# All expert weights from SP's queue, and a new order for the last third of a delta-rule and soft-MoE kernel

## The chip, the cores and the metric

The kernel runs on one core of one Trainium2 chip. The time is device microseconds of that core. Before the change three runs gave 293.0, 293.39 and 295.69 us, so the median is 293.39 us. One more execution was recorded by the hardware profiler; it took 296.5 us.

## The reference

Two blocks are computed one after the other, all in float32. The first is a delta-rule attention with a state of 48 by 48 for each of 4 x 8 heads, over 768 time steps:

```python
y[:, :, t] = np.einsum('bhd,bhde->bhe', q[:, :, t], state)
v_old = np.einsum('bhde,bhd->bhe', state, kt)          # kt: k normalised by its length
state = state + bt[:, :, :, None] * np.einsum('bhd,bhe->bhde', kt, vt - v_old)
```

Its output, laid out as 3072 rows of 384, is the input `x` of a soft mixture of 8 experts with 4 slots each:

```python
logits = x @ phi                                        # 3072 x 32
d = softmax(logits, axis=0); c = softmax(logits, axis=1)
slot_input = (d.T @ x).reshape(E, S_per_e, D)           # 8 x 4 x 384
for e in range(E):
    slot_out[e] = np.maximum(slot_input[e] @ w1[e], 0) @ w2[e]   # w1 384x1024, w2 1024x384
out = c @ slot_out.reshape(32, D)                       # 3072 x 384
```

The weights `w1` and `w2` are 12.58 MB each (8 x 384 x 1024 x 4 bytes).

## The kernel before, in words

**Tiling.** The 768 steps are cut into 12 chunks of 64 (n = 0 to 11). A chunk holds all 32 heads, with 64 time steps on each half of the 128 partitions. Two chunks form a pair g (0 to 5).

**Stages of a chunk.** `load` (L412) and `load_q` (L421) bring k, v and q in; a `load` is two operations of five DMAs each, one of 96 KB and four of 24 KB. `prep` turns k and q (L473) and forms the Gram blocks (L504). `invert(g)` inverts the triangular systems of a pair on VectorE and GpSimd: it starts with a spread (L563), runs 15 pairs of a multiplication and a subtraction (both recorded at the helper's line L277), and ends with two transposes, `back` (L626) and `backt` (L632). `join(g)` merges blocks with four products on TensorE, called p1 to p4 here (L716, L716, L761, L716), with copies between: `mask` (L687), `swap` (L671 on VectorE or GpSimd, L669 on ScalarE), `fix16` (L733), two `wide` (L739, L741), `zbadd` and `fix32` (L770).

**The recurrence.** `step(n)` scales v (`scale_v`, L277), multiplies k by the state (`ks`, L821), subtracts (`rest`, L827), and multiplies by the joined inverse (the product `w`, L840, interleaved with L782, the second half of the previous chunk's output). `uev` copies the result out of PSUM, `sup` (L867) adds it to the state and two `sev` copy the state to SBUF. `query` (L791) is the previous chunk's first half of output. `yev` copies a chunk's output to SBUF, `route` turns it (L902) and copies it. All copies out of PSUM stand at L281 when ScalarE does them and at L283 on VectorE. For n = 11 the second half of the output is a product of its own, `au` (L782 alone).

**Routing.** `pair(g)` forms the logits (`lg`, L920), a running maximum (L928 to L931), exponentials (L935), the slots' sums (L953, accumulated at L958), and the softmax over experts (L962 to L984). After the last pair a merge (L1050 to L1074) gives the slots' inputs `slb`.

**Experts and output.** `first(1)` and `first(0)` multiply by w1 (L1090, four groups of 24 matmuls), with relu (L1099) and transposes (L1106). `second(0)` and `second(1)` multiply by w2 for the two halves of the columns (L1123; eight groups of 16 matmuls each). After each half, `comb` (L1142) multiplies with the combine weights; a copy and a `put` (L1150) follow. A put is two DMAs of 96 KB; each half has 12 puts.

**What sets the order.** Nothing is scheduled at build time. Every function only records operations in a list (`pl.op`), numbered 0 to 1163. `Plan.run` then issues them in the order of the list `ORDER`, each on the engine that the string `ALTS` picks among the alternatives given to `pl.op`, and with its buffers at the columns of SBUF or the banks of PSUM that the list `PLACE` gives. So an engine's queue is the subsequence of `ORDER` that falls to it, and a later use of a column waits for the earlier one. The weights (25.2 MB) do not fit beside the attention's tiles, so most weight loads go to columns that an attention tile used before, and wait until its last reader is done.

**Weight loads.** w1 is 24 operations of two DMAs (256 KB each, L1029); w2 is 32 operations of two DMAs (192 KB each, L1040). Of the 56 operations 39 are issued on SP's queue and 17 on GpSimd's (POOL): w1 operations 1013, 1016, 1017, 1020, 1023, 1028, 1030, 1035 and w2 operations 1043, 1047, 1052, 1054, 1056, 1057, 1058, 1062, 1068. Six w2 operations go to columns that w1 of experts 4 to 7 held, and so wait for `first(1)`.

DMAs that SP and ScalarE issue share eight completion semaphores, taken in turn; a DMA waits until the eighth DMA before it has landed. GpSimd's DMAs have eight of their own.

Of the kernel before, what the change touches and what calls it, by code (L numbers as in the profile page):

```python
# [113 lines left out]
    "0010021211010001100200000000000000000001010000000000001000000000010000101000000000000000010100000011"  # L114
    "1000001000100001010000010100000000000110000000010000000110100000000211010100011000000000000000000000"
    "0000000000000000010000000000100000000001000000000000000000000111000000000100000011000010000000000011"
    "1100000000000000000000000000002022100001110110100000000000010000000000000000000000000000000100000000"
    "0000000100000000000000000000000000000000000011000000110100100010000000000000100100001000100000000010"
    "0000000000001100110010010000101000010000000100010000101011100010000010000000000000010000000000000000"
    "0000001010010012000000020011000000000000010201210010011000100002"  # L120
)


class Buf:


# [70 lines left out]
def kernel(  # L197
# [823 lines left out]
    for e in range(E):  # L1021
        for kk in range(NKT):
            w1b[e, kk] = t = done.pop(0) if done else pl.buf(F)
            pl.tag = ("w1", e)

            def go(q, e=e, kk=kk, t=t):
                s = moe_w1[e].rearrange("(p k) f -> p k f", k=NKT)
                for x in H2:
                    ENG[q].dma_start(out=A(t)[:, 512 * x:512 * x + 512], in_=s[:, kk, 512 * x:512 * x + 512])  # L1029
            pl.soft = [chain[8]]  # L1030
            pl.op(dq(0.8, 1.2, None), None, go, w=[t], bus=1.5, nd=2)
# [150 lines left out]
```

## Time and profile before

| | |
|---|---|
| median of the runs | 293.39 us |
| the profiled execution | 296.5 us, of which 294.8 us lie between its first and last instruction (the span) |
| PE (TensorE) busy | 227.0 us, 77% of the span, 6252 matmuls |
| DVE (VectorE) busy | 200.2 us, 68% |
| ACT (ScalarE) busy | 145.2 us, 49% |
| POOL (GpSimd) busy | 139.4 us, 47% |
| DMA | 45.13 MB, mean 153 GB/s |
| the chain that ended last | PE 39%, DVE 25%, issue 12%, ACT 9%, POOL 7% of the span |

The page gives times in microseconds from the span's first instruction. PEld is TensorE's weight load. A name with q (SPq, ACTq) is an engine's queue issuing a DMA. "Issue" in the chain is time in which an engine waited for nothing that the profile shows. A row of the chain reads: start, duration, engine, where the result goes, line, and the number of instructions merged. A row of the timeline adds the operation, the shapes, and in brackets the idle time before it with what ended it.

### The profile page before, as it was taken

The numbers are of one execution on the slowest core, as the hardware profiler recorded it, in microseconds if no ns is written. First come the engines' busy times: TensorE is split into PE (matmuls) and PEld (weight loads), VectorE is DVE, ScalarE is ACT, GpSimd is POOL, SyncE is SP. The second block draws the span as 40 slices with busy tenths as digits, with TensorE's granted clock in tenths as the row PEclk, the third lists the DMA queues.
The fourth block names the chain that finished last, engine by engine and source line by source line (L and its number), as shares of the span: only waits on it lengthen the run. The fifth ranks groups of instructions, "written<-read, shape, count | busy, mean of one in ns | idle before, by whom it ended". The sixth has DMA issues, their size and how long they took to land.

```text
span 294.8 us, 14440 instructions
## 1 busy us (share of the span) xinstructions
PE 227.0 (77%) x6252; PEld 183.3 (62%) x6252; DVE 200.2 (68%) x504; ACT 145.2 (49%) x325; POOL 139.4 (47%) x225
## 2 busy tenths in 40 slices
PE   0784788993879887798879977698756978999950
PEld 0563687872768776687667766576655864266640
DVE  4668979979877669778699889785664657113130
ACT  1253486784758356659736778473212432230321
POOL 8998468355483373226762545562730410200460
PEclk9997589999599999999999999999997999999985
DMA  8989642643432361335554607777795699990887
GB/s 138 159 153 188 103 79 59 120 79 58 84 61 52 59 113 24 59 63 117 128 93 111 168 5 226 193 195 221 208 362 186 199 359 374 349 332 4 219 224 201
DMA packets 81519, 45.13 MB, mean 153 GB/s; under 512 B 63520, under 2 KB 74704, under 8 KB 81456
## 3 DMA queue, kind: packets, MB, share of 16 engines
q1 hardware_dynamic: 72704, 30.28, 42.8%
q0 software_dynamic: 5232, 12.56, 15.7%
q10 hardware_dynamic: 3520, 1.38, 2.1%
q8 instruction: 49, 0.80, 1.2%
q14 instruction: 14, 0.11, 0.1%
HBM read 39.47 MB, written 4.72 MB: 150 GB/s over the span
## 4 chain that ended last, share of the span: by engine, by line
PE 39%; DVE 25%; issue 12%; ACT 9%; POOL 7%; DMA 3%; SPq 3%; DVEq 0%; POOLq 0%; ACTq 0%
DVE sb L277 9%; PE pb L716 6%; ACT sb L281 5%; POOL sb L277 5%; PE pb L473 4%; PE pb L1090 4%; PE pb L1123 3%; PE pb L504 3%; PE pb L902 3%; PE pb L782 2%; PE pb L821 2%; PE pb L791 2%; PE pb L867 2%; DMA sb<-in_k_dram 2%; DVE sb L283 2%
## 5 line engine op out<-in xcount | busy, mean ns | idle before, releaser
L281 ACT ACTIVATE sb<-pb 128x512 f32<-128x512 f32 (+5 forms) x144 | 76.0, 560 | 90.9 <-PE pb L473 23.2
L277 POOL TENSOR_TENSOR sb<-sb 128x256 f32<-128x256 f32 (+10 forms) x89 | 64.0, 728 | 66.8 <-DVE sb L277 33.9
L277 DVE TENSOR_TENSOR sb<-sb 128x126 f32<-128x126 f32 (+10 forms) x153 | 54.0, 355 | 11.2 <-POOL sb L277 6.8
L473 PE MATMUL pb<-sb 128*128 128x128 f32 x192 | 33.5, 323 | 15.1 <-DVE sb L329 8.1
L283 DVE COPY sb<-pb 128x512 f32<-128x512 f32 (+5 forms) x43 | 26.2, 618 | 26.0 <-PE pb L473 5.4
L473 PEld LDWEIGHTS pb<-sb 128*128 128x128 f32 x192 | 25.4, 164 | 19.5 <-issue 10.5
L716 PE MATMUL pb<-sb 64*64 64x64 f32 x1152 | 27.5, 232 | 12.3 <-DVE sb L277 4.7
L716 PEld LDWEIGHTS pb<-sb 64*64 64x64 f32 x1152 | 24.3, 144 | 16.0 <-issue 8.0
L504 PE MATMUL pb<-sb 64*64 64x128 f32 x768 | 27.2, 280 | 5.8 <-ACT sb L281 3.3
L840 PE MATMUL pb<-sb 64*64 64x48 f32 x768 | 26.5, 219 | 4.8 <-DVE sb L770 1.8
L840 PEld LDWEIGHTS pb<-sb 64*64 64x64 f32 x768 | 24.4, 135 | 7.6 <-DVE sb L770 2.4
L782 PE MATMUL pb<-sb 64*64 64x48 f32 x768 | 26.3, 219 | 2.2 <-issue 2.1
L504 PEld LDWEIGHTS pb<-sb 64*64 64x64 f32 x768 | 21.9, 136 | 9.1 <-ACT sb L281 4.7
L782 PEld LDWEIGHTS pb<-sb 64*64 64x64 f32 x768 | 24.2, 135 | 2.6 <-issue 2.5
L1040 POOL DMA_DIRECT2D sb<-in_moe_w_dram x18 | 9.7, 542 | 33.6 <-PE pb L953 16.1
L821 PE MATMUL pb<-sb 128*64 128x96 f32 x352 | 18.1, 250 | 3.6 <-ACT sb L281 1.3
L412 POOL DMA_DIRECT2D sb<-in_k_dram x35 | 19.6, 568 | 0.7 <-DVE sb L341 0.7
L1150 POOL DMA_DIRECT2D out_dram<-sb x14 | 8.4, 607 | 23.9 <-DVE sb L283 18.5
L513 ACT ACTIVATE sb<-pb,sb 128x128 f32<-128x128 f32 x48 | 17.0, 370 | 4.4 <-PE pb L504 4.1
L821 PEld LDWEIGHTS pb<-sb 128*64 128x64 f32 x352 | 15.5, 137 | 5.7 <-ACT sb L281 1.9
L791 PE MATMUL pb<-sb 128*64 128x96 f32 x352 | 17.4, 249 | 1.1 <-issue 0.5
L791 PEld LDWEIGHTS pb<-sb 128*64 128x64 f32 x352 | 15.2, 137 | 2.6 <-issue 1.0
(142 smaller groups left out, 379.3 us busy)
## 6 DMA issues: line engine op xcount, KB each, us to landing
sb<-in_moe_w_dram SPq DMA_DIRECT2D x46, 192.0 KB, 5.6
sb<-in_moe_w_dram SPq DMA_DIRECT2D x32, 256.0 KB, 4.1
sb<-in_moe_w_dram POOLq DMA_DIRECT2D x16, 256.0 KB, 5.0
sb<-in_moe_w_dram POOLq DMA_DIRECT2D x18, 192.0 KB, 5.7
sb<-in_q_dram SPq DMA_DIRECT2D x14, 192.0 KB, 4.2
out_dram<-sb SPq DMA_DIRECT2D x24, 96.0 KB, 3.3
sb<-in_v_dram SPq DMA_DIRECT2D x22, 96.0 KB, 3.4
sb<-in_v_dram SPq DMA_DIRECT2D x88, 24.0 KB, 3.0
```

The costliest lines, as they stand in the source:

```text
L277: ENG[e].tensor_tensor(*a, **kw)
L281: nc.scalar.activation(o, i, ACT.Copy)
L283: V.tensor_copy(o, i)
L412: ENG[e].dma_start(out=d()[p0:p0 + w, x], in_=s[t0:t0 + w, hs])
L473: nc.tensor.transpose(A(ps)[:, 0, P * j:P * j + P], A(src)[:, x:x + P], ident())
L504: mm(A(ps)[ha(r), c, P * j4:P * j4 + P].rearrange("p (a t) -> p a t", a=2), x[ha(c), j, r, 0], x[ha(c), j, r])
L513: nc.scalar.activation(o, gv()[:, z, :, 0, 32 * z:32 * z + 32], ACT.Copy, scale=M0() if z else M1())
L716: mm(A(ps)[ha(b), x, 64 * j:64 * j + RW].rearrange("p (a t) -> p a t", t=w), st, m)
L782: mm(pv(pY)[ha(1 - r), j // 4, j % 4, c], A(at)[ha(r), 512 * c + 64 * j:512 * c + 64 * j + 64], hv(u)[ha(r), j, c], start=first and c == 0 ...
L791: mm(A(pY)[ha(1 - r), j // 4, 96 * (j % 4):96 * (j % 4) + 96], kqv(KQ[n])[:, j, r, 1], Sv(n)[:, j, r], start=j % 4 == 0)
L821: mm(A(pR)[ha(r), j // 4, 96 * (j % 4):96 * (j % 4) + 96], kqv(KQ[n])[:, j, r, 0], Sv(n)[:, j, r])
L840: mm(pv(pW)[ha(r), j // 4, j % 4, c], A(zs)[ha(r), 64 * (zj * c + z0 + j):64 * (zj * c + z0 + j) + 64], hv(R)[ha(r), j, c])
```

## The change

Two lines change what a weight load may be issued on. The rest is a new `ORDER` from its position 811 on (of 1164), new `PLACE` columns for buffers of the later part, and new `ALTS` for 64 operations.

```diff
@@ w1 @@
             pl.soft = [chain[8]]
-            pl.op(dq(0.8, 1.2, None), None, go, w=[t], bus=1.5, nd=2)
+            pl.op([("SP", 0.8)], None, go, w=[t], bus=1.5, nd=2)
@@ w2 @@
             pl.soft = [chain[N - 1]]
-            pl.op(dq(0.8, 1.2, None), None, go, w=[t], bus=1.15, nd=2)
+            pl.op([("SP", 0.8)], None, go, w=[t], bus=1.15, nd=2)
@@ ORDER @@
-    683, 761, 791, 792, 793, 794, 681, 795, 684, 775, 931, 796, 902, 798, 799, 1021, 800, 801, 685, 802, 797,
-    830, 901, 903, 1030, 776, 904, 1020, 803, 804, 805, 806, 807, 808, 809, 810, 730, 905, 811, 812, 813, 814,
+    683, 761, 791, 792, 793, 794, 681, 795, 684, 775, 931, 796, 780, 902, 798, 799, 1020, 776, 800, 801, 802,
+    803, 901, 830, 804, 805, 806, 807, 863, 1021, 685, 808, 809, 810, 864, 811, 812, 903, 1030, 905, 904, 813,
...
```

`dq` offers SP and POOL; the new list offers SP alone. The main moves of the new lists, by operation:

| operation | before | after |
|---|---|---|
| 17 weight loads (34 DMAs) | POOL's queue | SP's queue, in the places where they stood or later |
| 1016 (w1, columns of the last q, turned by PE just before) | POOL | SP, one place ahead of the second half of v8 (898) and both halves of v9 (929, 930) |
| 946, first half of v10 | SP | POOL; v10's halves are 946 and 945 |
| 904 `yev` 7, 905 `uev` 8, on ACT | 904 first | 905 first |
| 907, 908, the two `sev` of step 8, on ACT | 907, then the copies 731, 864, 896, then 908 | 896, 731, then 907, 908 in a row |
| 798 to 807, the first ten products and subtractions of inversion 5 | 798 to 801 on POOL, the others on DVE behind `fix32` 685 of join 8 | 798, 800 and 804 to 807 on POOL; 799 and 801 to 803 on DVE ahead of 685; from 808 on DVE behind it |
| 895, the turn of route 6 on PE | between the query 933 and `lg` 865 of pair 2, which `back`'s partner `backt` 829 waits for | ahead of the state update 906; 865 follows 933 |
| 600, a mask of Gram block 8 (128x512) | DVE, right before `rest` 934 of step 9 | POOL |
| 832, 833, the swaps before p2 of join 10 | both DVE | 832 DVE, 833 ACT |
| 843, 844, the swaps before p4 of join 10 | both POOL | 843 DVE, 844 ACT |
| 893 `route` 6 on PE | right before p4 of join 10 | right after it |
| 950 `rest` of step 10, 712 and 713 of pair 1, on DVE | 950 ahead of `fix32`, 712 and 713 behind | all ahead of `fix32` of join 10 |
| 952 `yev` 9, 953 `uev` 10 | both DVE, 952 first | 952 ACT, 953 DVE |
| 955, 956, the two `sev` of step 10 | both ACT | 955 ACT, 956 DVE |
| 961, `lg` of pair 4 | after `au` of step 11 | between `ks` 980 and `w` 983 of step 11, behind 872 and 959 |
| 988 `yev` 11 | DVE | ACT |
| 990, 992, 994, 996, copies of routes 10 and 11 | all ACT | 992, 996 ACT; 990, 994 DVE |
| w2 loads that wait for `first(1)` | 6, of which 2 on POOL | 8, all on SP |
| 24 puts | 12 SP, 7 POOL, 5 ACT | 11 SP, 10 POOL, 3 ACT |
| last copy 1161 on ACT | behind two puts of the second half (1143, 1146) and followed by 1163 | behind one put (1151); nothing follows on ACT |

The operations themselves, their number and the arithmetic stay the same.

More of the change, by code (lines that the diff above doesn't have):

```diff
@@ L113 @@
     "0001000000000000000000000001011000001101000010001000010100000001000000200001011000001110000010000101"
[L114 to L120, printed above, removed]
+    "0010021211010001100200000000000000000001010000000000000000000000010000101000000000000000010100000011"
+    "0000001000100001010000010100000000000110000000010000000110100000000211010100011000000000000000000000"
+    "0000000000000000000000000000100000000001000000000000000000000110000000000100000010000010000000000010"
+    "1000111100000000000000000000002020101001110200100000000000010000000000000000000010000000000100100000"
+    "0000000100001000000000000000000000000000000011100000010110000000000000000000100000000000001000100010"
+    "0000000000000000000000000000000000000000000000000000000000000000000000000000000100000100000000000000"
+    "0000001100001012000100012011000000000000010000110102001000100001"
 )
```

76 rows, old and new, of tables (ORDER, PLACE) are left out of this document.

## Prediction

> **What bounds the kernel now.** I read the engine shares and the chain's summary first, then the table by stretch (start:end, length, busy us of PE, weight load, DVE, ACT and POOL, granted clock, DMA share, GB/s), and then the chain step by step where the order changes.
>
> ```profile
> DMA  8989642643432361335554607777795699990887
> ...
> q8 instruction: 49, 0.80, 1.2%
> ...
> sb<-in_moe_w_dram SPq DMA_DIRECT2D x46, 192.0 KB, 5.6
> ...
> sb<-in_v_dram SPq DMA_DIRECT2D x88, 24.0 KB, 3.0
> ```
>
> No engine bounds the whole (the chain's shares stand in the table above); the digits are the DMA's busy tenths in 40 slices of 7.37 us, and the last two rows give from issue to landing 5.6 and 3.0 us.
>
> ```profile
> 180.00:200.00 20.00, 15.26 (x491) 12.86 (x485) 16.60 (x47) 12.69 (x28) 9.49 (x19) 1.00 0.80 233
> 200.00:222.00 22.00, 15.45 (x613) 12.63 (x611) 12.95 (x25) 4.98 (x12) 9.44 (x13) 1.00 0.83 269
> ...
> 234.00:264.00 30.00, 27.17 (x368) 15.43 (x364) 13.03 (x50) 9.80 (x27) 4.79 (x9) 1.00 1.03 358
> ```
>
> In the recurrence PE is busy 15.45 of 22 us; in the experts 27.17 of 30 us, while the DMA runs at 358 GB/s. The chain from 208 on, start, duration and place:
>
> ```profile
> 208.95 1.20 PE pb L821 x23
> ...
> 212.12 1.09 PE pb L716 x64
> ...
> 215.53 1.69 issue
> ...
> 219.06 0.77 PE pb L920 x18
> 219.83 3.58 issue
> ...
> 224.02 0.41 PE pb L945
> ...
> 225.70 1.41 PE pb L867 x64
> 227.11 0.48 PE pb L902 x3
> ...
> 229.06 0.26 PE pb L962
> 229.32 1.47 PE pb L821 x32
> ...
> 231.27 0.78 PE pb L953 x8
> 232.05 0.18 PE pb L840
> ...
> 235.64 2.00 PE pb L782 x64
> ...
> 242.36 0.93 PE pb L920 x24
> ...
> 249.43 10.51 PE pb L1090 x96
> ...
> 262.38 6.00 PE pb L1123 x144
> ```
>
> PE works through its queue almost without a pause, except for the two stalls, so here the time is what stands on PE between a state and the next one.
>
> **The change part by part** (gain negative; each term is what reaches the next stage).
>
> *Inversion 5 and join 10, to the p4 product.*
>
> ```profile
> 185.68 1.41 DVE L770 SCALAR_TENSOR_TENSOR sb<-pb,sb 128x512 f32<-128x512 f32 x2 [1.03 <-PE pb L716]
> ...
> 187.28 7.36 DVE L277 TENSOR_TENSOR sb<-sb 128x78 f32<-128x78 f32 x25
> ...
> 196.55 1.25 DVE L632 STREAM_TRANSPOSE sb<-sb 128x1024 f32<-128x1024 f32 x1 [0.56 <-PE pb L920]
> ...
> 199.82 0.88 DVE L671 COPY sb<-sb 64x512 f32<-64x512 f32 x2
> ...
> 237.99 0.95 DVE L283 COPY sb<-pb 128x768 f32<-128x768 f32 x1
> ```
>
> ```profile
> 178.96 1.49 POOL L277 TENSOR_TENSOR sb<-sb 128x768 f32<-128x768 f32 x1
> 183.96 1.31 POOL L277 TENSOR_TENSOR sb<-sb 128x30 f32<-128x30 f32 x4 [3.51 <-DVE sb L277]
> ```
>
> Before, four products of the inversion end on POOL at 185.27 and the others begin on DVE only behind fix32 at 187.0; 25 of them take 7.36 us, 0.29 each. Now ten go ahead of or beside fix32. They change engine four times; with 0.33 us each on POOL (1.31 / 4) and a hand-over estimated at 0.1, the four on POOL end near 187.8, where DVE takes over the eleventh, which it now reaches at 188.7. That is 0.8 gained. fix32 itself starts 0.6 later, behind 803; step 8 has that slack, since its query is long done when `backt` ends. `backt` further waits 0.56 for the logits of pair 2, behind a turn that now stands earlier: 0.5 gained. The swaps before p2 take 0.88 on DVE in a row; split between DVE and ACT, 0.4. Then p1, p2 and, on PE behind p2, w of step 9 come 1.7 earlier, and so does ks of step 10 (208.95). A turn of 0.48 (the row at 227.11 shows the same three matmuls) goes behind p4: 0.5. Three small DVE operations and `rest` now stand ahead of fix32: 0.4 lost at most. In all **-1.9**; from 0 (POOL's hand-overs cost as much as they save) to -4 (all of it, and a stall beside it that falls away).
>
> *The update of step 10.* From the end of w (219.06) to `sup` (225.70) are 6.64 us, 3.58 of them a stall and 3.06 PE work. Behind w now stand turns, the logits and two small products, by the rows above 0.48 + 0.93 + 0.48 + 0.41 + 0.26 = 2.56: **-0.5**, with the stall kept as it is. `uev` on DVE alone, beside `yev` on ACT, is ready 0.95 after w, under this work. The two `sev` on two engines gain nothing: from `sup`'s end (227.11) PE is busy with a turn, the query and L962 up to 229.32, when `ks` starts.
>
> *The logits of pair 4 move ahead of w of step 11.* From `ks` (229.32) to w (232.05) are 2.73 us. Now 1.47 (`ks`) + 0.78 + 0.48 + 0.93 stand there, and between the last two an ACT copy of some 0.5: 4.2. **+1.5** lost.
>
> *From `au` to the logits of pair 5.* `au` ends at 237.64, the logits start at 242.36: 4.72 us.
>
> ```profile
> 240.67 1.64 ACT L281 ACTIVATE sb<-pb 128x384 f32<-128x384 f32 x4 [5.45 <-PE pb L902]
> ...
> 282.51 6.51 ACTq L1150 DMA_DIRECT2D out_dram<-sb  x4
> 289.15 0.81 ACT L281 ACTIVATE sb<-pb 128x768 f32<-128x768 f32 x1 [6.32 <-DMA out_dram<-sb]
> ```
>
> Now ACT copies `yev` 11 at once (0.81 by the last row, against 0.35 of waiting and 0.95 on DVE at 237.99), the logits of pair 4 (0.93) are gone, and the four copies (1.64 in a row) go to two engines. What stays is 0.9 for `yev`, two turns of 0.48 and a copy of 0.5 with hand-overs: 2.8. **-1.9**; the half of it if the copies on DVE queue behind its softmax.
>
> *The drain.*
>
> ```profile
> 153.84 10.34 SPq L412 DMA_DIRECT2D sb<-in_v_dram  x15
> ...
> 250.22 12.31 SPq L1040 DMA_DIRECT2D sb<-in_moe_w_dram  x18
> ...
> 271.57 20.43 SPq L1150 DMA_DIRECT2D out_dram<-sb  x24
> ```
>
> The last output copy on ACT starts at 289.15, 6.32 us idle behind puts that ACT's own queue issues over 6.51 us. Now one put stands before it, the copy runs near 286.5, and what follows goes elsewhere. SP then sets the end: its 24 output DMAs take 0.85 each; it has 22 now, 12 of them in the second half, from about 281.5, which at 0.70 to 0.85 end at 289.9 to 291.7, against 292.0. POOL takes six more. I take **-1.8**, between -0.3 (SP's pace holds) and -3 (ACT's wait was all of it).
>
> *The loads.* 34 DMAs come to SP. Two places matter. First, 1016 waits on SP for PE's last turn of q and holds 15 DMAs of v8 and v9 behind it, which issue now from 153.84 to 164.18, 0.69 each.
>
> ```profile
> 163.06 1.09 PE L473 MATMUL pb<-sb 128*128 128x128 f32 x8
> ```
>
> Held to 165, they end at 175.3, and with 3.0 of landing v9 is there at 178.3; POOL scales it at 178.96: free, with 0.7 to spare, and what it is later goes on to inversion 5. Second, from the end of w of step 11 SP still has 50 DMAs, 10.2 MB, to issue. At 358 GB/s that is 28.6 us; the last w2 product is due 31.0 after w (3.47 for query and `au`, 2.80 as above, 7.07 from these logits to `first`, 12.95 to `second`, and 4.67, seven ninths of its 6.00, from the starts in the chain). The margin is 0.4 if the last load needs 2 us more to land: I cost the loads at nothing, which is the least certain item here. POOL, free of 34 issues, gains nothing that is on the chain.
>
> Sum: -1.9 - 0.5 + 1.5 - 1.9 - 1.8 = -4.6. The profiled execution took 296.5, 3.1 more than the median 293.39; by that median I predict **288.8**. Its own range, with each term at its bounds half correlated, is 285.5 to 291.5.
>
> **The rivals.**
>
> *SP's queue sets the end of the experts.* For it: 18 loads take 12.31 us on SP, 0.68 each, in a stretch where POOL issued others; 50 would take 34.2 us. With 5.6 of landing that is up to 8.8 behind what is due, so up to 298; with half of that slip 3.8 too late: 292.6. Against: the DMA was saturated in that stretch, so the pace of 0.68 may be the memory's, not the queue's. It decides from the point where the last load lands later than 31.0 after w.
>
> *PE's stalls grow: slower.* On the whole chain stand
>
> ```profile
> 53.47 3.54 issue
> ...
> 120.83 2.23 issue
> ...
> 187.61 2.69 issue
> ```
>
> and in the last third 1.69 and 3.58, right in or behind the products w and L782 of 128 short matmuls, as 187.61 is. The instruction queue q8 brought 49 blocks, 0.80 MB, so 16 KB each, and these waits fit blocks that come late. For the products of steps 7 to 11 the last three rows sum to 8.0; if SP's loads, now denser up to 234, hold up each of the five by the 3.58 that two stalls reach, it is 17.9: +9.9, so 298.7 with the gains. For it: at 0.80 and 0.83 of DMA share there are three such stalls in 42 us (2.69, 1.69, 3.58). Against: 53.47 and 120.83 stand in slices of 0.6 and 0.3 by the DMA line of the page, so the share alone does not make them. The Trainium skill, "Runtime: NRT & Kernel Launch", section "Instruction fetch mechanics", says that the next block is fetched while the current one runs and that crossing a 16 KiB boundary is mostly hidden; by that rule the stalls would be no fetches, and this rival would not exist. The 3.58 us without any wait shown speak against the rule here.
>
> *The stalls shrink.* If POOL's loads are what holds the instruction blocks up, half of these 8.0 us goes: 4.0 more, 284.8. The Trainium skill, "DMA: Bandwidth & Descriptors", section "Queues, rings and completion order", says that an engine alternates between the queues it has work for, packet by packet, so one queue fewer would serve the instruction queue sooner; no run here shows it yet.
>
> That the change does not do what it says is ruled out: the built order has every weight load on SP.
>
> **How the numbers follow.** Forecast 0.45; SP's queue 0.22 (290.5 to 298); more stalls 0.20 (292 to 302); fewer stalls 0.13 (281 to 287). A measurement here can tell about 1%, so faster is below 290.5 and slower above 296.3. Faster: 0.40 of the forecast and 0.13: 0.53. Within 1%: 0.05 of the forecast, 0.17 of SP's queue, 0.03 of the stalls: 0.25. Slower: 0.05 + 0.17 = 0.22. The range from 283.5 to 298 leaves out some 0.06 below and 0.10 above. Cases of both signs hold much of the chance; the likeliest one's own range is the one above.
>
> **What would show it.** Right: `backt` 1.3 earlier without PE in its bracket; p4 followed, not preceded, by a turn; some 4.2 from `ks` to w and 2.8 from `au` to the logits in step 11; `first` near 246.5; no ACT idle of 6 us before its last copy; `first` and `second` as dense as now. Wrong: issue rows over 2 us that were not there; PE waiting for DMA at L1090 or L1123; POOL waiting for v9 near 179; SP's last put no earlier than 292.

## The result and the profile after

The changed kernel takes 292.01 us in the median of 18 runs; the kernel before, run beside it, 294.24 us. The ratio is 0.9909 with a 95% interval of 0.988 to 0.9938; it leaves out the executions that took over 1.5% longer than the fastest of their kernel. So the gain is 2.2 us by the medians and some 2.7 us by the ratio, where 4.6 were forecast. The direction was right, the size was not.

The two profiles at hand differ by more (span 294.8 before, 290.0 after), and that is the first thing to learn from this case: one profile of this kernel is a sample. A second profile of the changed kernel has a span of 295.2, two more of the kernel before 294.8 and 297.1. So stages are compared below as means over the profiles (three of before, two of after), each stage between the first instructions of its lines, in microseconds.

| stage | before | after | difference | forecast |
|---|---|---|---|---|
| start to the spread of inversion 5 | 178.8, 177.7, 177.2 | 175.9, 176.9 | -1.5 | 0 |
| spread to `back` | 15.9, 16.8, 16.5 | 16.1, 16.2 | -0.3 | -0.8 |
| `back` to w of step 10 | 20.2, 20.8, 20.8 | 19.2, 22.6 | +0.3 | -1.1 |
| w of step 10 to w of step 11 | 17.0, 17.3, 18.7 | 15.4, 15.3 | -2.3 | +1.0 |
| w of step 11 to the first product with w1 | 17.4, 17.2, 17.1 | 15.2, 15.0 | -2.2 | -1.9 |
| products with w1 | 10.5, 10.5, 12.0 | 12.2, 12.2 | +1.2 | 0 |
| products with w2 | 15.4, 15.4, 15.4 | 16.9, 18.3 | +2.2 | 0 |
| their end to the end | 17.0, 16.7, 17.0 | 16.7, 16.5 | -0.3 | -1.8 |

The differences sum to -3.0 (the 2.4 us between the products with w1 and those with w2 are the same in both). From the spread to the first product with w1 it is 4.5 us less, where 2.8 were forecast, and the products of the experts take 3.4 us more.

That looks as if the order gained more than it should. It did not. PE's issue waits (times in which it waited for nothing that the profile shows) from 176 to 262 us sum to 11.0, 10.5 and 12.5 us before and to 6.2 and 5.5 after. Without them the way from the spread to the first product with w1 takes 59.6, 61.6 and 60.6 us before, 59.7 and 63.5 after: it is no shorter. It also holds stretches in which PE was granted half its clock: 3.4, 6.8 and some 7 us of them before, 3.4 and 10.2 after. A row of the second profile of the changed kernel shows 6.8 us of it inside the stage from `back` to w, which took 22.6 us there and 19.2 in the first profile:

```profile
201.70:208.50 6.80, 5.92 (x151) 4.27 (x155) 2.26 (x4) 2.00 (x3) 1.44 (x2) 0.50 0.37 114
```

(Columns as in the prediction's table by stretch; the third from the end is the granted clock.)

The table by stretch of the kernel after (columns as in the prediction; the last row is one that was cut for the first product with w1):

```profile
180.00:200.00 20.00, 16.35 (x589) 13.87 (x588) 16.36 (x41) 10.61 (x24) 9.63 (x18) 1.00 0.77 229
200.00:222.00 22.00, 18.07 (x600) 14.85 (x594) 12.96 (x24) 7.37 (x17) 7.85 (x6) 0.92 0.77 239
...
234.00:264.00 30.00, 28.40 (x331) 14.16 (x329) 9.47 (x36) 7.06 (x22) 0.00 (x0) 0.94 0.90 311
...
242.00:246.00 4.00, 4.00 (x24) 0.98 (x20) 2.93 (x14) 0.51 (x2) 0.00 (x0) 0.57 1.06 368
```

From 200 to 222 PE is busy 18.07 us where it was 15.45, at a granted clock of 0.92 where it was 1.00. In the experts DMA brings 311 GB/s where it brought 358, with GpSimd (POOL) idle, and PE starts the product with w1 at a granted clock of 0.57. The chain of the kernel after, from the same place as before:

```profile
208.25 1.09 PE pb L716 x64
209.34 0.48 PE pb L902 x3
...
214.62 2.13 issue
...
217.97 1.32 PE pb L867 x64
...
222.55 1.47 PE pb L821 x32
...
225.86 0.86 PE pb L920 x24
226.72 0.18 PE pb L840
...
234.89 1.16 PE pb L920 x24
...
238.21 4.70 DMA sb<-in_moe_w_dram
242.97 4.76 DMA sb<-in_moe_w_dram
247.76 3.96 DMA sb<-in_moe_w_dram
251.75 4.68 DMA sb<-in_moe_w_dram
256.44 5.21 DMA sb<-in_moe_w_dram
261.69 2.14 PE pb L1123 x34
```

The steps of the prediction can be read in it: the turn behind p4 instead of ahead of it, the logits of pair 4 (225.86) ahead of w, the logits of pair 5 at 234.89. Then comes what it did not have: from 238 to 261 the chain is no longer PE but a row of weight loads, each waiting for an earlier one, up to a matmul of the product with w2.

### The profile page after: what moved, and what is told of

Read it like the earlier page. It is cut to its first block, busy times and chain, and to the rows that moved or that the text cites. A ratio compares the mean times of both kernels' runs of the same rounds, so it can differ in the third digit from the quotient of the medians.

```text
span 290.0 us, 14451 instructions
## 1 busy us (share of the span) xinstructions
PE 228.2 (79%) x6252; PEld 182.5 (63%) x6252; DVE 194.9 (67%) x498; ACT 146.8 (51%) x327; POOL 132.1 (46%) x206
## 3 DMA queue, kind: packets, MB, share of 16 engines
HBM read 39.47 MB, written 4.72 MB: 152 GB/s over the span
## 4 chain that ended last, share of the span: by engine, by line
PE 34%; DVE 28%; DMA 10%; issue 10%; ACT 7%; POOL 5%; SPq 2%; ACTq 1%; POOLq 0%; DVEq 0%
DVE sb L277 12%; DMA sb<-in_moe_w_dram 8%; PE pb L716 7%; POOL sb L277 5%; PE pb L473 4%; PE pb L504 4%; ACT sb L281 3%; PE pb L1142 3%; PE pb L1123 2%; DMA sb<-in_k_dram 2%; PE pb L902 2%; PE pb L791 2%; PE pb L821 2%; DVE sb L626 2%; PE pb L840 2%
## 5 line engine op out<-in xcount | busy, mean ns | idle before, releaser
L277 POOL TENSOR_TENSOR sb<-sb 128x256 f32<-128x256 f32 (+10 forms) x95 | 69.9, 747 | 79.8 <-DVE sb L277 34.8
L277 DVE TENSOR_TENSOR sb<-sb 128x110 f32<-128x110 f32 (+10 forms) x147 | 51.1, 350 | 11.9 <-POOL sb L277 7.8
L473 PE MATMUL pb<-sb 128*128 128x128 f32 x192 | 32.6, 318 | 15.5 <-DVE sb L326 7.8
L283 DVE COPY sb<-pb 128x512 f32<-128x512 f32 (+5 forms) x42 | 24.9, 597 | 26.5 <-PE pb L473 7.4
L473 PEld LDWEIGHTS pb<-sb 128*128 128x128 f32 x192 | 24.8, 162 | 19.9 <-issue 11.9
L1150 POOL DMA_DIRECT2D out_dram<-sb x20 | 12.0, 606 | 51.9 <-DVE sb L283 47.1
L840 PE MATMUL pb<-sb 64*64 64x48 f32 x768 | 25.9, 220 | 2.9 <-DVE sb L770 1.6
L782 PE MATMUL pb<-sb 64*64 64x48 f32 x768 | 26.1, 220 | 0.5 <-issue 0.5
L513 ACT ACTIVATE sb<-pb,sb 128x128 f32<-128x128 f32 x48 | 16.8, 367 | 4.1 <-PE pb L504 3.9
L821 PEld LDWEIGHTS pb<-sb 128*64 128x64 f32 x352 | 15.2, 137 | 4.8 <-ACT sb L281 1.5
L791 PEld LDWEIGHTS pb<-sb 128*64 128x64 f32 x352 | 15.8, 142 | 3.0 <-DVE sb L733 0.8
L867 PE MATMUL pb<-sb 64*48 64x48 f32 x704 | 11.8, 213 | 1.8 <-issue 1.3
```

What stands on the lines that cost most here:

```text
L277: ENG[e].tensor_tensor(*a, **kw)
L283: V.tensor_copy(o, i)
L473: nc.tensor.transpose(A(ps)[:, 0, P * j:P * j + P], A(src)[:, x:x + P], ident())
L513: nc.scalar.activation(o, gv()[:, z, :, 0, 32 * z:32 * z + 32], ACT.Copy, scale=M0() if z else M1())
L782: mm(pv(pY)[ha(1 - r), j // 4, j % 4, c], A(at)[ha(r), 512 * c + 64 * j:512 * c + 64 * j + 64], hv(u)[ha(r), j, c], start=first and c == 0 ...
L791: mm(A(pY)[ha(1 - r), j // 4, 96 * (j % 4):96 * (j % 4) + 96], kqv(KQ[n])[:, j, r, 1], Sv(n)[:, j, r], start=j % 4 == 0)
```

## The experiments

**The same kernels once more.** Three runs without an edit.

> The kernel before, profiled once more, to see what of the difference between the two profiles is a difference between executions. Theory A (the 2.9 us by which the changed kernel's profile is ahead at the spread of inversion 5, where both orders are still the same, are stalls of PE that fall differently in each execution): the spread starts between 175.5 and 178.5 here, not at 178.8, and at least one of the issue rows over 1.5 us at 53, 120, 187 and 219 is gone or stands elsewhere. Theory B (they come from the loads that left GpSimd's queue): the spread starts within 0.7 of 178.8 again.

> The changed kernel, profiled once more. Theory A: the spread of inversion 5 starts anywhere from 175.5 to 179, and the first groups of the product with w1 run at full clock (10.5 us in all) or at half clock for their first 24 matmuls (12.2) as the stretch of half clock falls. Theory B: the spread starts within 0.7 of 175.9 again.

> The kernel before, a third profile: the product with w1 in 10.5 by theory T's twin for before (its late loads are split too, 28 on SP and 6 on GpSimd), 12.2 if the half clock there falls by chance; sum of PE's issue waits from 176 to 262 us 9 to 12, as in the two others, or 5 to 8 if they scatter as they do with all loads on SP (5.5 to 9.9).

Measured: the spread of inversion 5 at 177.7, 177.2 and 176.9; the products with w1 in 10.5, 12.0 and 12.2 us. In the other profiles of this study it starts between 175.5 and 178.8, and the latest of them with all loads on SP at 178.8 too. So the 2.9 us by which the first profile of the changed kernel was ahead there are mostly a difference between executions: theory A, though with three profiles of before a rest of about one us can't be told from a difference. The half clock at the product with w1 is met in before too (12.0 us).

**Each part alone.** First the queue, with the order of before:

```diff
-            pl.op(dq(0.8, 1.2, None), None, go, w=[t], bus=1.5, nd=2)
+            pl.op([("SP", 0.8)], None, go, w=[t], bus=1.5, nd=2)
 (w2 likewise; ORDER, PLACE as before; ALTS 0 for the 17 loads)
```

> The order, the columns and the engines of before, with the 17 loads on SP's queue in the places where they stood: the first part of the change alone. Theory A (the new order brings the gain, the queue costs): ratio 0.998 to 1.012, since v8 and v9 wait behind a load and the last w2 loads come later; the last of them issues after 262. Theory B (loads that leave GpSimd bring the gain ahead of inversion 5): the spread near 176 and a ratio near 0.99.

Measured: 0.9967 (0.9922 to 1.0012), not to be told from no change. The spread came at 176.5, as theory B has it, but the ratio is in neither theory's range. The last load was issued at 257.0, not after 262 as theory A had it, and the products with w2 took 15.4 us, without a wait. From spread to `back` it took 14.6 us, in the old order, against 15.9 to 16.8 in before; that is taken up below. Then the order, with the 17 loads on GpSimd:

```diff
-            pl.op([("SP", 0.8)], None, go, w=[t], bus=1.5, nd=2)
+            pl.op(dq(0.8, 1.2, None), None, go, w=[t], bus=1.5, nd=2)
 (w2 likewise; ORDER, PLACE as after; ALTS 1 for the 17 loads)
```

> The order and the columns of the changed kernel, with the 17 loads on GpSimd's queue again: the second part alone. Theory A: the recurrence gains as in the changed kernel (from the spread of inversion 5 to the first product with w1 some 66 us, against 70.6 before), no wait for w2 stays in the product with w2, ratio 0.985 to 0.992. Theory B: the spread near 178.8, ratio 0.995 to 1.0.

Measured: 1.0065 (1.002 to 1.011), slower than before by more than its interval. Neither theory had that: the two parts are not a gain and a cost that add. With the loads on GpSimd the order is a loss; whether it is a gain over the loads alone on SP (0.9909 to 0.9967) the intervals leave open. Theory A also said that no wait for w2 would stay here. It stayed, with GpSimd carrying 17 of the loads:

```profile
265.50 1.17 PE L1123 MATMUL pb<-sb 128*32 128x192 f32 x20 [0.64 <-DMA sb<-in_moe_w_dram]
```

The products with w2 took 16.7 us, against 15.4 in before and in the run with the loads alone, and 16.9 and 18.3 in the changed kernel. So that wait comes with the new order first. On SP alone it is longer in the mean, 2.5 us in five profiles of the new order against 1.2 in five with some of the loads on GpSimd (this one and the four of the split below), but the two groups overlap. One reason for the loss stands in GpSimd's timeline of this run:

```profile
181.23 0.24 POOL L277 TENSOR_TENSOR sb<-sb 128x30 f32<-128x30 f32 x1 [3.51 <-DVE sb L277]
181.68 1.11 POOL L1029 DMA_DIRECT2D sb<-in_moe_w_dram  x2 [0.21 <-issue]
182.81 0.29 POOL L277 TENSOR_TENSOR sb<-sb 128x56 f32<-128x56 f32 x1
```

The new order lets GpSimd and VectorE take turns in the inversion, and a load that takes GpSimd 1.11 us to issue stands between two of the turns: spread to `back` is 17.3 us here, 16.1 in the changed kernel. PE's issue waits are 9.8, as in before. Against the changed kernel (16.1 us, and issue waits of 6.2 and 5.5) these two are some 5 us in this one profile; how they share the 1.6% between the two versions was not tried apart.

**The mask on GpSimd.** From spread to `back` the order gained less than the ten products moved ahead should give. VectorE and GpSimd of the kernel after:

```profile
183.00 1.41 DVE L770 SCALAR_TENSOR_TENSOR sb<-pb,sb 128x512 f32<-128x512 f32 x2
185.06 6.00 DVE L277 TENSOR_TENSOR sb<-sb 128x120 f32<-128x120 f32 x16 [0.66 <-POOL sb L277]
```

```profile
183.26 3.00 POOL L277 TENSOR_TENSOR sb<-sb 128x96 f32<-128x96 f32 x5 [0.97 <-PE pb L791]
```

The hand-over came as forecast, 9.1 us behind the spread where the same product stood at 9.9 before. But the 16 products on VectorE take 6.00 us, 0.38 each, not 0.29. The first one of them takes 1.33 (1.33 again in the second profile); beside it, from 184.98 to 186.26, GpSimd runs the fifth operation of its group, the mask 600, which the change moved to it. The mask went back:

```diff
 ORDER
-    814, 815, 816, 600, 895, 896, 1015, 817,
+    814, 815, 816, 895, 896, 1015, 817,
-    826, 827, 828, 829, 834, 835, 934,
+    (the same, with 600 right before 934)
 ALTS[600]: POOL -> DVE
```

> The changed kernel with one operation put back: 600, a mask of 128x512 on GpSimd for 1.28 us, goes to VectorE again, right before rest of step 9. Theory P (while it runs, VectorE's first product of the inversion behind the hand-over takes 1.33 us in place of 0.29, since both engines want the same operands' path): that product takes 0.3 again, from the spread of inversion 5 to back are 15.1 us instead of 16.1, less 0.0 to 0.7 for the mask itself on VectorE; the total is 0.3 to 1.0 us under the changed kernel's 292.0. Rival: the product waits for something else, the 1.33 stays and the mask costs 0.7 more.

The same group there:

```profile
184.53 4.95 DVE L280 TENSOR_TENSOR sb<-sb 128x120 f32<-128x120 f32 x16 [0.66 <-POOL sb L280]
```

4.95 for 6.00, and 14.8 us from spread to `back`: theory P. The Trainium skill, "SBUF — State Buffer", section "SBUF: two separate sides", says that a VectorE operation with two inputs in SBUF and a GpSimd operation that reads SBUF need the same pair of ports, and that whichever starts first holds it for its whole length while the other waits. The product has two inputs in SBUF, the mask reads SBUF; the mask starts 0.08 us ahead of the product, and the product ends 0.14 us behind the mask, so the trace agrees. In the total the repair does not show: 0.9883 (0.9826 to 0.9941) to before, its interval over that of the changed kernel.

How much was there to gain in this stage? The old order with all loads on SP (`loads_only`):

```profile
182.05 1.40 DVE L770 SCALAR_TENSOR_TENSOR sb<-pb,sb 128x512 f32<-128x512 f32 x2
...
183.65 7.37 DVE L277 TENSOR_TENSOR sb<-sb 128x78 f32<-128x78 f32 x25
```

Here `fix32` (L770) does not wait for PE; in the three profiles of before it waited 1.03, 1.91 and 1.60 us for the last product of join 8. Without that wait the old order needs 14.6 us from spread to `back` (14.9 and 14.8 in the two twins below), the new one 16.1 and, with the mask back on VectorE, 14.8. So taking turns gains only where PE is late with that product; otherwise it gains nothing, and the mask makes it a loss.

**The late loads on two queues.**

```diff
 w1, w2: dq(0.8, 1.2, None) again; ORDER, PLACE as after
 ALTS 1 (POOL) for 1031, 1029, 1032, 1038, 1065, 1060, 1049, 1037, 1053, 1062, 1056, 1067
```

> The changed kernel with 12 of its last 25 loads, every second one from operation 1031 on, on GpSimd's idle queue. Theory Q (SP's own pace, 0.585 us for each of its last 38 loads, makes the product with w2 wait): the loads end some 3 us earlier, the pitch of the product's matmuls stays at 0.041 us throughout (7.4 us for its first half becomes 6.1), total 1.0 to 1.5 under the changed kernel. Theory M (the memory's rate of 330 to 360 GB/s and the bytes that the new order leaves for the end): the wait shrinks by 0.4 at most. If stalls of PE come from GpSimd's queue at any time, they would not grow here, since the last short products are over by 234.

The first 144 matmuls of the product with w2 in the kernel after and in this one (PE's timeline):

```profile
256.39 4.75 PE L1123 MATMUL pb<-sb 128*32 128x192 f32 x110 [0.19 <-ACT sb L281]
261.69 2.14 PE L1123 MATMUL pb<-sb 128*32 128x192 f32 x34 [0.55 <-DMA sb<-in_moe_w_dram]
```

```profile
255.74 6.35 PE L1123 MATMUL pb<-sb 128*32 128x192 f32 x144 [0.20 <-ACT sb L281]
```

The first 144 matmuls take 6.35 us in one piece instead of 7.44 with a wait. The stretch from 242 to 258 of the kernel after and of its second profile, then of the two profiles with the split:

```profile
242.00:258.00 16.00, 15.81 (x154) 6.54 (x150) 4.57 (x17) 4.21 (x9) 0.00 (x0) 0.89 1.02 351
```

```profile
242.00:258.00 16.00, 15.25 (x119) 5.33 (x118) 6.08 (x25) 2.59 (x8) 0.00 (x0) 0.89 0.94 316
```

```profile
242.00:258.00 16.00, 15.65 (x175) 7.93 (x179) 5.03 (x19) 4.21 (x9) 7.02 (x13) 1.00 1.04 374
```

```profile
242.00:258.00 16.00, 15.25 (x135) 6.56 (x132) 6.43 (x26) 3.51 (x12) 8.36 (x16) 1.00 1.05 377
```

SP alone brings 351 and 316 GB/s here, SP and GpSimd together 374 and 377, and in this first profile the wait shrinks by more than the 0.4 us that theory M allows. That speaks for theory Q. But SP's queue can do more than 351. In the last experiment below, with all loads on SP, the same stretch shows

```profile
242.00:258.00 16.00, 15.25 (x131) 5.43 (x123) 6.81 (x27) 3.17 (x11) 0.00 (x0) 0.95 1.03 368
```

and before has 362 to 368 there. So 351 is no limit of SP's queue, and what keeps it lower in the changed kernel was not found. The ratio is 0.9882 (0.9824 to 0.994), again not to be told from the changed kernel's 0.9909 by the intervals. A second profile had the wait again:

> The changed kernel with every second late load on GpSimd, profiled once more. Two profiles with late loads so split had the product with w1 in 10.5 us; twelve others but the two of before had it in 11.8 to 12.2, with PE at half clock for 3.4 us from its first matmuls. Theory T (the half clock there hangs on how the late loads are split): 10.5 again. Rival (it falls by chance, by what PE did in the 20 us before): 12.2.

The products with w1 took 10.5 us, those with w2 17.7 (15.8 in the first): the split does not always end the wait, since from w of step 11 to the first product with w1 this order needs only 15 us and the loads come no sooner for it.

**Both repairs.** The mask on VectorE and the split together.

> The changed kernel with both repairs: the mask 600 on VectorE right before rest of step 9, and every second of the last 25 loads on GpSimd. If the two gains add (1.05 us less from the spread of inversion 5 to back, and 1.4 us less in the product with w2, each seen alone), the ratio to before is 0.981 to 0.988; if stalls of PE take up what is gained earlier, 0.988 to 0.992, as each repair alone and the changed kernel have it.

Measured: 0.9861 (0.9787 to 0.9936) to before. In its profile the products with w2 took 17.4 us, so the wait stood there too. It is the lowest ratio of all versions tried and lies where gains that add would put it, but its interval reaches over that of the changed kernel, so a better version is not shown.

> The version with both repairs, profiled once more. Theory T: the product with w1 takes 10.5 again; rival: 12.2. The product with w2, 15.8 and 17.4 in the two profiles with the split and 16.8 to 19.0 in five without: 15.4 to 16.5 if the split takes the wait away for good, over 17 if loads still come late when step 11 is early.

12.2 us for the product with w1, so theory T falls: the half clock there is not tied to the split. (Ten earlier profiles had it, not the twelve that the expectation counts.) The products with w2 took 15.6; but they began 1.7 us later for the half clock ahead of them, which gave the loads that time.

**PE's issue waits.** Two twins of the kernel before, with 17 loads on one queue cut to 16 columns:

```diff
-                    ENG[q].dma_start(out=A(t)[:, Dm * x:Dm * x + Dm], in_=s[:, 2 * tp + x])
+                    n = 16 if (e, tp) in T2 else Dm
+                    ENG[q].dma_start(out=A(t)[:, Dm * x:Dm * x + n], in_=s[:, 2 * tp + x, 0:n])
 (w1 likewise; T1, T2 name GpSimd's 17 loads, or 17 of SP's)
```

> The kernel before, where the 17 loads on GpSimd's queue bring 16 columns each instead of 512 or 384 (their weights are then not those of the reference): the queue is used as often, and 8 MB of the 45 are gone. The sum of PE's waits of kind issue from 176 to 262 us was 11.3 and 10.5 in two profiles of before, 6.2, 5.5 and 7.1 with all loads on SP. Theory R1 (bytes in GpSimd's queue delay PE's instruction blocks): 5 to 7.5 here, and 9 to 12 in the twin, where 17 loads on SP's queue are cut. Theory R2 (any bytes on the 16 DMA engines do): 5 to 7.5 in both. Theory R3 (the issue of GpSimd's DMAs as such, its descriptors): 9 to 12 here.

> The twin: the kernel before, where 17 loads on SP's queue from the same stretch (8 of w1, 9 of w2, so the same bytes) bring 16 columns each, and GpSimd's 17 stay whole. Sum of PE's issue waits from 176 to 262: by theory R1 9 to 12, by R2 5 to 7.5, by R3 9 to 12.

The waits of PE from 176 to 262 us (line, what it waited for, us in total, times, longest) of the kernel before:

```profile
PE pb L920 <- issue: 3.6, 1, 3.6
PE pb L782 <- issue: 2.1, 2, 1.7
...
PE pb L716 <- issue: 1.1, 1, 1.1
PE pb L867 <- issue: 1.0, 1, 1.0
...
```

and of the two twins, GpSimd's loads cut and SP's cut:

```profile
PE pb L867 <- issue: 1.4, 1, 1.4
PE pb L782 <- issue: 1.1, 1, 1.1
PE pb L920 <- issue: 1.1, 1, 1.1
...
```

```profile
PE pb L920 <- issue: 3.9, 1, 3.9
...
PE pb L821 <- issue: 0.5, 1, 0.5
...
```

Over all rows of kind issue 11.0 becomes 4.4 and 5.6 (7.5 of the 45 MB are gone in each): fewer bytes on the DMA engines shorten these waits, whichever queue they leave (R2, though 4.4 is under the 5 to 7.5 it named). Each twin has one profile, so this rests on 4.4 and 5.6 lying below the 9.8 to 12.5 of all four profiles with full loads of which 17 are on GpSimd. That is not all of it. With the same bytes the sum is 9.8 to 12.5 in those four, and 5.5 to 9.9 in twelve with no load on GpSimd in the recurrence, 11.0 and 7.7 in the mean. So moving the loads off GpSimd seems worth some 3 us of issue waits, about the third rival of the prediction. But the two groups differ in their orders too: three of the four have the old order (10.5 to 12.5, against 7.1 and 9.0 with the loads on SP), and the one with the new order, 9.8, lies within the range of those without. By which way a queue would matter was not found.

**The drain.** The last two puts of SP, four DMAs, on another queue:

```diff
 ALTS[1155], ALTS[1162]: SP -> POOL   (first run)
 ALTS[1155], ALTS[1162]: SP -> ACT    (second run)
```

> The changed kernel with the last two puts of SP (4 DMAs) on GpSimd. From the end of the product with w2 to the end are 17.0 and 16.7 us in two profiles of before, 16.7 and 16.5 in two of the changed kernel. Theory S (SP's own issue of 12 DMAs in the second half sets the end): 15.0 to 15.8 here. Theory L (the DMAs in flight, eight per pool of semaphores, set the pace; SP and ACT share one pool, GpSimd has its own): 15.0 to 16.0 here, but no gain in the twin with ACT. Theory C (the last copy and its puts, 281.8 to 289 in the changed kernel, set it): 16.5 or more.

> The twin: the same two puts on ACT, behind its last copy. Theory S: 15.0 to 15.8 from the end of the product with w2 to the end. Theory L: 16.4 to 17.0, since SP and ACT wait for the same eight. Theory C: 16.5 or more.

From the end of the products with w2 to the end: 19.3 us with GpSimd, 16.3 with ACT, 16.5 and 16.7 without the edit. On ACT there is no clear gain, though SP's last put is issued 3.6 us earlier against that point. 16.3 lies in no theory's range; it is far from S and just under L and C, so SP's own issue does not set the end, and what does stays open. The run with GpSimd decides nothing, since an ACT put of the first half took 2.5 us there and held up ACT's copies behind it:

```profile
274.68 3.13 ACTq L1150 DMA_DIRECT2D out_dram<-sb  x2
277.86 0.32 ACT L1128 COPY sb<-pb 128x192 f32<-128x192 f32 x1 [3.20 <-DMA out_dram<-sb]
```

**The engines of `yev` and the routes alone.**

```diff
 (loads_only, and:) ALTS[988]: DVE -> ACT;  ALTS[990], ALTS[994]: ACT -> DVE
```

> The order and columns of before, all loads on SP, and of the new order only this: yev of step 11 on ACT, and two of the four copies of routes 10 and 11 on VectorE. Theory A (the stretch from w of step 11 to the first product with w1, 17.5 us with the order of before and 15.0 with the new one, owes its 2.3 us to these engines and to the logits of pair 4): 16.2 to 17.0 for this stretch here, ratio 0.990 to 0.996. Rival (this gain is met by loads that are not there or by the half clock of PE at the first product with w1): ratio 0.994 to 1.0.

0.9929 (0.9881 to 0.9977). It is not to be told from the 0.9967 of the loads alone. Its profiled execution took 296.1 us, among the longest of its twelve, so its stages are not read (the stretch that theory A speaks of took 19.0 there): inconclusive.

**The logits of pair 4 back behind `au`.**

```diff
 ORDER
-    872, 1045, 924, 959, 960, 961, 1052, 781, 982, 983, 1036, 1040, 877, 873, 962, 985, 1046, 984, 869, 963, 1050,
+    872, 1045, 924, 959, 960, 1052, 781, 982, 983, 1036, 1040, 877, 873, 985, 984, 869,
 (961, 1046, 1050, 962, 963, 964 behind 988)
```

> The changed kernel with the logits of pair 4 (operations 961 to 964) behind au and yev of step 11 again, and the two loads that take their tiles' columns (1046, 1050) behind them. By the prediction's terms, from w of step 10 to w of step 11 it is 1.5 less (15.4 becomes 13.9), and from w of step 11 to the first product with w1 0.9 to 1.5 more (15.0 becomes 16.0 to 16.5). Rival (the move costs nothing, since PE waits for something else there): both stretches stay within 0.5 of the changed kernel's, apart from what stalls and half clock make.

From w of step 10 to w of step 11 it is 12.9 us (15.4 with the move), from there to the product with w1 19.9 (15.0). The first of these differences is partly clock: the changed kernel has one stretch of half clock in that stage, this run none. Two profiles of the changed order that have none there either (the first with the split, the second with both repairs) need 12.2 and 12.1 us without issue waits, this run 10.7. So the move costs 1.5, as the prediction worked out, and from `ks` to w it is 4.17 us where before has 2.73. In the second stage this run has a stretch of half clock, which makes up to 1.7 of the 4.9, and 0.8 of issue waits; some 2.4 us stay, more than the 1.5 at most that was expected. The logits of both pairs now stand in one stretch:

```profile
235.84 0.92 PE pb L923 x24
...
239.68 0.98 PE pb L923 x24
```

And the products with w2 take 22.5 us. The loads 1046 and 1050 wait for the tiles that these logits read (L923 is their line here), and all loads behind them on SP's queue wait with them:

```profile
SPq L1043 <- PE pb L923: 5.2, 1, 5.2
```

That is a reason for the move that the prediction did not see: it frees the columns for the loads. It also shows how near to the edge the loads are.

## Why the prediction was off, step by step

The step that failed first is the loads, costed at nothing: they made the products with w2 2.2 us longer. Next to it the drain gained 0.3 instead of 1.8. And of the 2.8 us that the order was to gain up to the experts, no sign is left once issue waits are taken out; the 4.5 us that are gained there are issue waits, which no term of the sum had. That the total came out on the forecast's side of zero is owed to these waits, not to the mechanism that was forecast; one of the rivals had them.

- **The loads, costed at nothing: failed; +2.2.** The sum had the last load there 30.6 us behind w of step 11 (28.6 to bring the bytes, 2 to land) and its product due at 31.0. In the two profiles the last load was issued 28.8 and 30.5 us behind the end of w and landed 5.1 and 4.6 us later, at 33.9 and 35.0. The product with w2 began at 27.7 and 27.5; with the 4.67 us of the prediction its last weights were due at 32.3 and 32.1. They were 1.6 and 2.9 late, and the product took 1.5 and 2.8 longer than in before. So the pace of SP was nearly as counted, 0.585 us for each of these loads against 0.57:

```profile
235.57 22.23 SPq L1040 DMA_DIRECT2D sb<-in_moe_w_dram  x38
```

What was mis-sized is the time from issue to landing: 2 us, where the prediction's own row gave 5.6. The price of missing the margin stood among the rivals with 3.8 (half of its 8.8 would be 4.4). That rival's mechanism, SP's queue, is only a part: with 17 loads on GpSimd the new order still lost 1.2 us here, and the old order with all loads on SP lost nothing.

- **The drain, -1.8: mis-sized; -0.3,** the end of the range where "SP's pace holds". ACT's idle time ahead of its last copy did fall from 6.32 to 3.02 us, but that copy did not set the end. SP's 22 DMAs took 20.07 us, 0.91 each, where the sum had 0.70 to 0.85. Moving four of them to ACT brought no clear gain, so the queue's own issue is not what holds it; what does is not shown.
- **Inversion 5 and join 10, -1.9: failed in its first half.** From spread to `back` 0.3 was gained, not 0.8. The hand-over and `backt` came as worked out (9.1 for 9.9 us to the eleventh product, and no wait of `backt` for PE in the bracket: 192.06 + 1.25 to 193.44). What failed is the line of the change that the step costed at nothing, the mask on GpSimd: 1.05 us on VectorE's chain. The step also took the start of `fix32` as given, which in before was late by a wait for PE; without that wait the old order is as fast (14.6 us) as the new one with the mask put back (14.8). From `back` to w of step 10 the first profile after is 1.4 us shorter than the mean of before, near the 1.1 forecast; the second is 2.0 longer, with 6.8 us at half clock where the others have none. The twins of before with fewer bytes have 18.8 and 18.5 us there, less than the 19.2 of the changed kernel, so that the order makes this gain is not shown.
- **Update of step 10 and the logits of pair 4, -0.5 + 1.5 = +1.0: the second term right, the first not.** The stage gained 2.3 us, because its stalls fell from 5.3, 4.0 and 5.8 us to 2.1 and 2.1. "With the stall kept as it is" was the one wrong part that helped. As work, it lost more than forecast: without issue waits, and in profiles without half clock in this stage, it takes 9.9 and 10.2 us in the old order (the loads alone, and the twin with GpSimd's loads cut) and 12.2 and 12.1 in the new one. The 3.06 us of PE work between w and `sup` that the -0.5 was worked out from stood partly at half clock, which the row of that stretch, of before, shows (0.86 is the granted clock; from 223.5 to 226.9 it was 0.50):

```profile
222.00:234.00 12.00, 10.59 (x284) 8.51 (x284) 7.07 (x20) 4.24 (x13) 1.59 (x3) 0.86 0.51 162
```

In the same profiles at full clock this work is 2.04 us in the old order and 2.40 in the new.

- **From `au` on, -1.9: right, a little more.** From `au` to the logits of pair 5 it is 2.10 us in both profiles, after 4.72, 4.45 and 4.39; the whole stage up to the product with w1 is 2.2 shorter.
- **What no step had: PE's clock.** The product with w1 starts at half clock (0.57 from 242 to 246) in 12 of 18 profiles, up to 1.7 us each. The Trainium skill, "TensorE: Matmul & The Clock Gate", section "HAM oscillation — how this bites in real kernels", says that a gap of PE across a window of 3.4 us lowers the clock at the next burst. In the recurrence a trace agrees: in before PE did nothing from 220.0 to 223.4, and half clock followed at 223.5 (in the changed kernel it followed a stall of 2.1 us as well). But ahead of the product with w1 no trace shows such a gap. The last 3.4 us before it, in before, where full clock followed, and in the changed kernel, where half clock followed:

```profile
246.00:249.40 3.40, 2.65 (x18) 1.73 (x18) 2.31 (x12) 0.95 (x4) 0.00 (x0) 1.00 1.06 370
```

```profile
238.40:241.80 3.40, 2.68 (x19) 1.71 (x18) 1.76 (x9) 0.50 (x3) 0.00 (x0) 1.00 1.05 384
```

PE was busy 2.65 and 2.68 us of them, so what decides there stays open.

- **The rivals.** Fewer stalls (0.13) happened, and so did the loads' wait (0.22); more stalls (0.20) did not. They were priced as if one excluded the other, and here two came together: some -5 us of issue waits in these profiles, +2.2 of waits for loads.

## What to carry to other kernels

When an order is written out by hand and engines take turns, an operation that is moved to an "idle" engine has to be looked at for what runs beside it, not only for its own queue. When a change makes one stage earlier, price the transfers that the next stage needs with the measured time from issue to landing, and take a margin under a microsecond as a wait. A gap that one profile shows ahead of an operation can be a stall and not the order's fault: look at it in a second execution before a new order is built to fill it. And where executions differ by 2% and a change is worth 1%, compare stages over several profiles, and take issue waits and the granted clock out of them, before any of them is explained.

## What the runs showed of the hardware

- A product of 128x120 on VectorE that takes 0.28 us alone took 1.33 in both profiles while GpSimd ran a 128x512 product for 1.28.
- From 242 to 258 us SP's queue alone brought 351 and 316 GB/s of weight loads in the changed kernel and 368 with the logits moved back; SP and GpSimd together brought 362 to 368 in before and 374 and 377 with the late loads split.
- PE's waits without a shown cause in the recurrence's fast matmul stretches fell from 11.0 us to 4.4 and 5.6, one profile each, when 7.5 MB of loads were cut, whichever queue they were on.
- A stretch of half clock of 3.4 us fell on the same product in some executions of one program (12.0 us) and not in others (10.5).
